# Strassen's scheme for feed-forward's first product of two blocks, in place of the output product of three

## The chip, the cores and the metric

The kernel runs on one core of a Trainium2 chip. The metric is the device time of one execution in microseconds (us), as the median of several runs. PE is the matrix engine, PEld its weight loads, DVE, ACT and POOL are the three elementwise engines, and SP issues the DMAs. PSUM is the accumulator memory that PE writes: 8 banks of 512 fp32 columns by 128 partitions. SBUF is the working memory.

## The reference

```python
attn_out = _attn_ref(q, k, v, f)            # 4 batches, 8 heads, 576 tokens, head size 64, decayed causal
x = attn_out.transpose(0, 2, 1, 3).reshape(2304, 512)
h = x @ w_in                                # 512 -> 2048       "feed-forward's first product"
g = np.maximum(0.01 * h, h)
x = g @ w_out                               # 2048 -> 512
h = x @ w_in2                               # 512 -> 1024       "layer 2"
e = np.exp(h - h.max(-1)); sm = e / (e.sum(-1) + 1e-09)
solu = h * sm
ln = (solu - mean(solu)) / sqrt(var(solu) + 1e-06) * g_ln
out = ln @ w_out2                           # 1024 -> 512       "the output product"
```

## The kernel before, in words

The 2304 tokens are 9 blocks of 256 (`TB`). Every product that has to be near fp32 is made of three fp16 matmuls: each operand is split into a high half and the rest, and high·high, high·low and low·high are summed in PSUM.

**Stages.** Attention runs over 16 pairs of heads. Feed-forward (`ffn`, L1056) takes one block and one half `g` of the hidden units: `hidden` (L1022) makes one 512-column PSUM bank per `k` (8 `k` in all, 4 in each half) with 24 matmuls of 256 columns, ACT and DVE make the activation and its two fp16 halves out of it, and then 4 times 24 matmuls of 256 columns make this half's share of `g @ w_out`, which is added into a tile `yo` and at last stored to HBM. `load_y` (L1091) reads such a block back and splits it, `layer2` (L1117) makes seven Strassen products out of it (L1124; 6 matmuls of 512 columns each) into the PSUM tiles `ph` (two banks each; two of them in all) and `ps_g`, and `normal` (L1166) does softmax and layer norm for each half `e` of the block (128 tokens): exp, a multiplication with its sum, a square with its sum, four small POOL instructions (`rstd`, L1183), an affine step.

**The output product** has two forms. The plain one (L1199 to L1218) splits the 128 normalised tokens, transposes the 2048 halves by one DMA, and runs 24 matmuls of 512 columns (`layer2_out`). For the last three blocks in order (`MIXED`, L87) `layer2_mix` (L1229) uses Strassen's scheme instead: both halves of the block are the rows, sums of their quarters are made on DVE and POOL, seven pieces are split and transposed by a DMA of 1024 each, and seven products of 12 matmuls of 256 columns are made (L1258) and combined by seven additions on DVE (L1275) after one copy on ACT (L1280). Its weights are mixed once, in `mixed_o` (L1002), on DVE, POOL and ACT.

**What sets the order.** The program is written as operations with a priority, a cost and the buffers they use (`Plan`, L148). `Plan.run` plays them against its cost table and writes out, for each engine, one fixed order of instructions; an operation that names several engines is given to one of them there. Constants such as `ORDER` (the order in which the blocks reach layer 2), `L2P`, `OUTP`, `PASSES` and `LD` are priorities or parts of them. Buffers have tags (`ps_f`: three PSUM banks; `ph`; `wz`: SBUF tiles of 128 by 512 fp32), and a tag that is no longer needed hands its tiles to another (`heirs`). On the chip each engine runs its order strictly, and waits where an input or a buffer isn't free.

Lines that many groups share are helpers: L529 is every matmul, L483, L488 and L490 are copies on ACT, DVE and POOL (`copy_on`), L494, L497 and L498 subtractions or additions (`sub_on`), L520 DMAs, L526 DMA transposes.

Of the kernel before, what the change touches and what calls it, by code (L numbers as in the profile page):

```python
# [30 lines left out]
ORDER = (0, 4, 1, 5, 3, 2, 6, 8, 7)  # L31
# [6 lines left out]
PASSES = (("A", 0, 127.52, 0.5), ("A", 1, 162.84, 3), ("B", 0, 200, 3.07), ("A", 2, 222, 8), ("B", 1, 234.49, 20), ("A", 3, 338, 8), ("B", 2, 372.93, 20), ("B", 3, 454.38, 15.2))  # L38
# [5 lines left out]
LD = -0.77  # L44
# [15 lines left out]
NWY = 12  # L60
NY2 = 2
NHL2 = 2
NTR = 3
PWL = 500.0
DMAR = 298.92
YB_ENGS = ("ACT",)
# [19 lines left out]
LNS = 256.0  # L86
MIXED = (6, 7, 8)  # L87
OMP = 931.77
# [37 lines left out]
WEIGHT2 = {"DVE": 1.93}  # L126
# [14 lines left out]
S_ENGS = ("POOL",)  # L141
O_ENGS = ("DVE", "POOL")
C_ENGS = ("ACT",)
NR2 = 1
# [266 lines left out]
def body(tc, kqa, kq, vt, f, wa, w2i, w2o, gln, out):  # L411
# [521 lines left out]
    def load_wi(k, prio):  # L933
# [7 lines left out]
        inverse(WS + k, ev(EK + k), ("w", k), ("k", k), prio)  # L941
# [114 lines left out]
    def ffn(blk, g, prio):  # L1056
        eprio = prio - EP
        first, last = blk not in YO, LEFT.setdefault(blk, 2) == 1
# [6 lines left out]
        gs = {k: hidden(k, XB[blk], prio + HST * i, eprio + i) for i, k in enumerate(GRP[g])}  # L1065
        for q in range(2):
            ps, yo = P.buf("ps_f"), YO[blk][q]
            for d in range(2):
# [6 lines left out]
                P.op(PE, 6 * len(GRP[g]) * mmr(TB), pe, prio + YD + 4 * q + 2 * d, r=list(gs.values()) + [WO[2 * k + i] for k in GRP[g] for i in range(2)],  # L1075
# [15 lines left out]
    def load_y(blk, prio):  # L1091
        yw, sy, y = P.buf("yw"), P.buf("sy"), P.buf("y2")
# [16 lines left out]
        pieces = [(512 * e, 512, lambda e=e: four(yw.t[:, 0:1024])[:, e::2], (yw, "e%d" % e)) for e in range(2)] + [(1024, 768, lambda: four(sy.t), sy)]  # L1109
        for at, n, v, k in pieces:  # L1110
            copy_f(lambda at=at, n=n: four(y.t[:, 0, at:at + n]), v, n, prio, scale=lambda: ev(IY + blk), w=[(y, (0, at))], r=[k, (EX, ("iy", blk))])
        for at, n, v, k in pieces:
            sub_f(lambda at=at, n=n: four(y.t[:, 1, at:at + n]), v, lambda at=at, n=n: four(y.t[:, 0, at:at + n]), n, prio, scale=lambda: ev(IY + blk),
                  w=[(y, (1, at))], rw=[k], r=[(y, (0, at)), (EX, ("iy", blk))])
        return y

    def layer2(tb, y, prio, oprios):  # L1117
# [7 lines left out]
        def prod(p, at, n, pr):  # L1125

            def pe():
                for k in range(2):
                    yh, yl = (y.t[:, j, at + 128 * k:at + 128 * k + 128] for j in range(2))
# [5 lines left out]
            P.op(PE, 6 * mmr(512), pe, pr, r=[y, W2I[0, n], W2I[1, n]], w=[p])  # L1135
# [24 lines left out]
        E = []  # L1160
# [249 lines left out]
```

## Time and profile before

| | |
|---|---|
| median of 3 runs | 749.15 us (748.75 to 750.18) |
| the profiled execution | 748.48 us, of which its span is 746.7 us |
| PE busy | 694.7 us, 93% of the span, 5711 matmuls |
| DVE, ACT, POOL busy | 534.6, 527.8, 393.6 us (72%, 71%, 53%) |
| mean granted clock of PE | 0.991 |

The span goes from the first to the last instruction; the 1.8 us between it and the execution's time lie outside. Matmuls overlap in the records (one of 256 columns is shown with 273 ns, but 24 of them in a row take 2.62 us), so the price of a matmul is read from a run of them, and not from its mean duration. A busy engine is not a bound one: what PE waits for, and where, is read from the waits and from the timeline.

### The profile page before, as it was taken

The page shows a single profiled execution, that of the slowest core. Times are in us where ns is not written, and L with a number is a line of the kernel's source. Part 1 is how long each engine was busy: PE and PEld are TensorE (multiplying, and loading weights), DVE is VectorE, ACT ScalarE, POOL GpSimd, SP SyncE. Part 2 cuts the span into 40 slices and gives each one's busy share as a digit, 9 for nine tenths or more (in the row PEclk, how much of TensorE's full clock was granted, in tenths as well). Part 3 has the DMA queues.
Part 4 walks back from the last instruction along what each step waited for, and adds up shares of the span by engine and source line. Part 5 has one row for each costly group of instructions (what it writes and reads, how often), then busy time and mean ns, then how long its engine had stood idle before and what let it go on. Part 6 is the DMA issues. An engine that isn't in the chain of part 4 may idle for free. (4 is left out here: it accounts for less than half of the span.)

```text
span 746.7 us, 15980 instructions
## 1 busy us (share of the span) xinstructions
PE 694.7 (93%) x5711; PEld 545.0 (73%) x5711; DVE 534.6 (72%) x1423; ACT 527.8 (71%) x1212; POOL 393.6 (53%) x503
## 2 busy tenths in 40 slices
PE   3368699999999999999999999999999999999997
PEld 2246488888888878888879888688856565444665
DVE  6998878888868787777975873341766774577873
ACT  4789989997988599989895754232744754457771
POOL 4557879794462075647521881020455865157661
PEclk9999699999999999999999999999999999999999
DMA  7999678647566675775965322010211335143666
GB/s 222 288 235 274 127 215 220 166 87 169 140 138 147 112 176 109 125 135 139 194 120 150 129 87 84 1 58 1 79 37 57 82 75 141 58 113 72 123 146 141
DMA packets 173599, 96.56 MB, mean 129 GB/s; under 512 B 153920, under 2 KB 153936, under 8 KB 173520
## 3 DMA queue, kind: packets, MB, share of 16 engines
q1 hardware_dynamic: 173488, 95.53, 54.2%
q8 instruction: 45, 0.74, 0.4%
q14 instruction: 34, 0.28, 0.1%
q10 hardware_dynamic: 32, 0.02, 0.0%
HBM read 47.95 MB, written 10.06 MB: 78 GB/s over the span
## 5 line engine op out<-in xcount | busy, mean ns | idle before, releaser
L529 PEld LDWEIGHTS <-wz 128*128 128x128 f16 x2904 | 281.4, 98 | 42.4 <-issue 6.7
L529 PE MATMUL ps_f<-g,wz 128*128 128x256 f16 x768 | 102.9, 276 | 0.0
L494 DVE SCALAR_TENSOR_TENSOR hl<-ps_s,st,hl 128x512 f16<-128x512 f32 (+4 forms) x160 | 82.1, 538 | 19.8 <-ACT hl L483 18.5
L529 PE MATMUL ps_f<-dec,wz 128*128 128x256 f16 x744 | 91.7, 273 | 0.0
L749 ACT ACTIVATE ps_s<-ps_s,st 128x512 f32<-128x512 f32 (+4 forms) x160 | 78.4, 490 | 13.2 <-DVE st L802 10.6
L498 POOL TENSOR_TENSOR kq<-raw,kq 64x576 fp32r<-64x576 f32 (+1 forms) x63 | 77.8, 1239 | 10.6 <-DMA pt<-hl 3.4
L483 ACT ACTIVATE hl<-ps_s,st 128x512 f16<-128x512 f32 (+4 forms) x153 | 74.8, 528 | 5.3 <-issue 1.6
L529 PE MATMUL ps_v<-pt,VT 128*128 128x128 f16 (+1 forms) x928 | 60.9, 217 | 18.9 <-DVE xr L836 12.3
L529 PEld LDWEIGHTS <-qa 128*128 128x128 f16 x696 | 67.5, 98 | 10.1 <-issue 1.4
L529 PEld LDWEIGHTS <-VT 128*128 128x128 f16 x928 | 53.5, 101 | 25.2 <-issue 9.4
L529 PE MATMUL ps_f<-x,wz 128*128 128x256 f16 x582 | 71.6, 276 | 0.0
L802 DVE CUSTOM_DVE_ANT_0 ps_s<-ps_s,mask 128x512 f32<-128x512 f32 (+3 forms) x128 | 62.4, 497 | 10.9 <-PE ps_s L529 9.1
L529 PEld LDWEIGHTS <-y 128*128 128x128 f16 x378 | 36.8, 98 | 45.7 <-issue 4.0
L529 PE MATMUL ps_s<-kq 128*128 128x512 f32 (+5 forms) x256 | 62.5, 375 | 0.9 <-DVE hl L494 0.4
L529 PEld LDWEIGHTS <-tr 128*128 128x128 f16 x348 | 33.9, 98 | 33.1
L529 PE MATMUL ps_f<-sd,wz 128*128 128x256 f16 x360 | 49.1, 273 | 0.0
L529 PEld LDWEIGHTS ps_s<-kq 128*128 128x128 f32 (+1 forms) x256 | 42.6, 197 | 6.7 <-DVE hl L494 1.0
L529 PE MATMUL ps_f<-wst,wz 128*128 128x256 f16 x366 | 47.1, 273 | 0.0
L836 DVE SCALAR_TENSOR_TENSOR xr<-ps_v,xr 64x256 f32<-64x256 f32 (+1 forms) x96 | 33.9, 353 | 14.8 <-ACT xr L833 13.2
L1037 ACT ACTIVATE ps_f<-ps_f 128x512 f32<-128x512 f32 x72 | 42.5, 590 | 0.3
L1038 DVE TENSOR_TENSOR g<-ps_f,g 128x512 f16<-128x512 f32 x40 | 27.5, 688 | 19.1 <-ACT ps_f L1037 18.8
L1038 DVE TENSOR_TENSOR dec<-ps_f,dec 128x512 f16<-128x512 f32 x32 | 22.0, 688 | 23.7 <-ACT ps_f L1037 23.2
(346 smaller groups left out, 1473.2 us busy)
## 6 DMA issues: line engine op xcount, KB each, us to landing
wst<-wa SPq DMA_DIRECT2D x32, 512.0 KB
raw<-kq SPq DMA_DIRECT2D x16, 480.0 KB
VT<-vt SPq DMA_DIRECT2D x16, 320.0 KB
raw<-yp_d SPq DMA_DIRECT2D x18, 256.0 KB
raw<-w2i SPq DMA_DIRECT2D x8, 512.0 KB
raw<-w2o SPq DMA_DIRECT2D x8, 512.0 KB
out<-ot SPq DMA_DIRECT2D x16, 256.0 KB
raw<-kqa SPq DMA_DIRECT2D x12, 256.0 KB
```

The source lines that it names most:

```text
L483: nc.scalar.activation(o, i, CP, scale=1.0 if scale is None else scale)
L494: nc.vector.scalar_tensor_tensor(o, a, scale, b, op0=ALU.mult, op1=ALU.subtract)
L498: (nc.vector if eng == DVE else nc.gpsimd).tensor_tensor(o, a, b, op=op)
L529: nc.tensor.matmul(o, lhsT=l, rhs=r, start=start, stop=stop)
L749: P.op(ACT, act(W, 1, True) + 93, lambda view=view, j=j, k=k: nc.scalar.activation(view(), view(), AF.Exp, bias=sts.t[:, j:j + 1], scale=- ...
L802: P.op(DVE, dve(W) + 130, lambda i=i, j=j, view=view: nc.vector.tensor_tensor_reduce(view(), view(), mask[:, 512 - 128 * i:640], -0.125, 3 ...
L836: P.op(DVE, dve(n) + 60, lambda: nc.vector.scalar_tensor_tensor(xr.t[a:a + 64, dst0:dst0 + n], ps.t[a:a + 64, c0:c1], PS, xr.t[a:a + 64, d ...
L1037: P.op(ACT, act(512, 0, True), lambda: nc.scalar.activation(ps.t, ps.t, AF.Prelu, scale=GS, alpha=0.01), eprio, rw=[ps])
L1038: P.op(DVE, dve(512) + 60, lambda: nc.vector.tensor_tensor(g.t[:, 1], ps.t, g.t[:, 0], op=ALU.subtract), eprio, w=[(g, 1)], r=[ps, (g, 0)])
```

## The change

Feed-forward's first product of blocks 6 and 7, which the order puts last, is made for both blocks together by Strassen's scheme (`hidden2`): the blocks are the two rows, the two halves of the 512 inputs the columns. Per `k` seven products of 6 matmuls of 256 columns replace 2 times 24 matmuls. One copy on ACT and seven additions on DVE combine them in one `ph` tile, and activation and split follow for each block. The weights' mixtures (`mixed_w`, per `k`) and the blocks' (`mixed_x`, once) are made ahead on DVE, POOL and ACT. `layer2_mix` and `mixed_o` are gone: the output product is plain for all nine blocks.

Tiles follow: `wt` holds the mixed weights and later becomes the tiles of the normalised halves and their transposes; `y2` becomes two tags; the second-layer weights are loaded after the last mixture is made (`deps`). Block 8 moves ahead of 6 and 7, and 1 ahead of 4. Some priorities and engine choices differ. Power-of-two scales differ too (`TOP2`, `GS`, `LNS`), which changes no instruction's size.

```diff
-ORDER = (0, 4, 1, 5, 3, 2, 6, 8, 7)
+ORDER = (0, 1, 4, 5, 3, 2, 8, 6, 7)
-... ("A", 2, 222, 8) ...
+... ("A", 2, 222, 9.78) ...
-LD = -0.77
+LD = 3.77
-NWY = 12
+NWY = 3
-YB_ENGS = ("ACT",)
+YB_ENGS = ("DVE", "ACT")
-MIXED = (6, 7, 8)
+PU = (((6, 7), 1), ((6, 7), 0))
-S_ENGS = ("POOL",)
+S_ENGS = ("DVE", "POOL")
...
-    def mixed_o(c, prio, after):
...
+    def mixed_w(k, prio, after):
+        za, zb, n, t = P.buf("wz"), P.buf("wz"), P.buf("wz"), P.buf("wt")
+        half = lambda z, h: lambda: z.t[:, 256 * h:256 * h + 256]
+        for z, c in ((za, 2 * k), (zb, 2 * k + 1)):
+            sub_f(lambda z=z: z.t, lambda c=c: W(WI[c], 0), lambda c=c: W(WI[c], 1), 512, prio, M_ENGS, op=ALU.add, w=[z], r=[WI[c]], deps=after)
+        sub_f(half(n, 0), half(zb, 1), half(zb, 0), 256, prio, M_ENGS, w=[(n, 0)], r=[zb])
...
+    def hidden2(k, p, prio, eprio):
+        X, Y, Z, u, ga, gb = P.buf("ps_f"), P.buf("ps_f"), P.buf("ph"), P.buf("hr"), P.buf("g"), P.buf("g")
...
+            def pe(o=o, xt=xt, w=w):
+                for d in range(2):
+                    wh, wl = (w(j)[:, 128 * d:128 * d + 128] for j in range(2))
+                    xh, xl = (xt()[:, j, TB * d:TB * d + TB] for j in range(2))
+                    mm(at(o)(), wh, xh, d == 0, False)
+                    mm(at(o)(), wh, xl, False, False)
+                    mm(at(o)(), wl, xh, False, d == 1)
...
+        plus(u2, P6, r1, w=[u2], r=[bank(P6), r1])
+        plus(u3, C22, u2, w=[u3], r=[bank(C22), u2])
+        plus(u2, P5, u2, rw=[u2], r=[bank(P5)])
+        plus(C22, P5, u3, rw=[bank(C22)], r=[bank(P5), u3])
+        plus(C21, C21, u3, rw=[bank(C21)], r=[u3])
+        plus(C11, C11, r1, rw=[bank(C11)], r=[r1])
+        plus(C12, C12, u2, rw=[bank(C12)], r=[u2])
+        for e, g in ((1, gb), (0, ga)):
...
+            P.op(ACT, act(512, 0, True), lambda g=g, row=row: nc.scalar.activation(g.t[:, 0], row(), AF.Prelu, scale=GS, alpha=0.01), eprio, w=[(g, 0)], r=ks)
+            P.op(ACT, act(512, 0, True), lambda row=row: nc.scalar.activation(row(), row(), AF.Prelu, scale=GS, alpha=0.01), eprio - 0.5 - 0.1 * e, rw=ks)
+            P.op(DVE, dve(512) + 60, lambda g=g, row=row: nc.vector.tensor_tensor(g.t[:, 1], row(), g.t[:, 0], op=ALU.subtract), eprio, w=[(g, 1)], r=ks + [(g, 0)])
...
     def load_w2i(k, h, prio):
         j = 2 * k + h
-        z = ZI[j] = whole(w2i[k, h], prio)
+        z = ZI[j] = whole(w2i[k, h], prio, None, mixed[-1:])
...
-            E.append(normal(2 * tb + e, blk, p, st, eprio, oprios[e], tb not in MIXED))
-        if tb in MIXED:
-            layer2_mix(tb, E[0], E[1], oprios[0], eprio)
+            normal(2 * tb + e, blk, p, st, eprio, oprios[e])
...
-    def layer2_mix(tb, e1, e2, oprio, eprio):
```

The change moves instructions on every engine. First VectorE, in the middle of feed-forward. Before, at the second half of block 7, these rows stand there: one 512-wide subtraction per `k` (L1038), among splits of the output weights (L494).

```order
L494 SCALAR_TENSOR_TENSOR wz_70<-wy_5612,ex,wz_70 128x512
L494 SCALAR_TENSOR_TENSOR wz_72<-wz_78,ex,wz_72 128x512
L1038 TENSOR_TENSOR dec_102<-ps_f_167,dec_102 128x512
L494 SCALAR_TENSOR_TENSOR wz_78<-wy_5613,ex,wz_78 128x512
L1038 TENSOR_TENSOR g_103<-ps_f_166,g_103 128x512
L494 SCALAR_TENSOR_TENSOR wz_75<-wst_98,ex,wz_75 128x512
L1142 ISA ph_5607,s_5636<-ph_5607,wst_99 128x512
L1142 ISA s_5636 128x1
L1038 TENSOR_TENSOR g_104<-ps_f_168,g_104 128x512
```

Now, at the pair of blocks 6 and 7 (L1105 is an addition of `hidden2`, 256 wide, out of PSUM; L1119 the subtraction; `hr` its partial sums):

```order
L1119 TENSOR_TENSOR dec_102<-ph_5562,dec_102 128x512
L1119 TENSOR_TENSOR dec_101<-ph_5562,dec_101 128x512
L1105 TENSOR_TENSOR hr_5584<-ph_5563,hr_5584 128x256
L1105 TENSOR_TENSOR hr_5584<-ps_f_168,hr_5584 128x256
L1105 TENSOR_TENSOR ph_5563<-ps_f_168,hr_5584 128x256
L1105 TENSOR_TENSOR ph_5563<-ph_5563,hr_5584 128x256 x3
L497 SCALAR_TENSOR_TENSOR wz_72<-qa,ex,wz_72 128x512
L1119 TENSOR_TENSOR g_106<-ph_5563,g_106 128x512
L1119 TENSOR_TENSOR g_103<-ph_5563,g_103 128x512
```

So a `k` of the pair has nine rows where two single blocks had two, and they come in a chain. The second place is POOL, just ahead of layer 2's first product, where the low halves of its mixed weights are made (two rows each: a scaling, L500, and a subtraction, L501). Ten such pairs stand there nearly in a row; four of them:

```order
L500 TENSOR_SCALAR wst_98<-wst_98,ex 128x512
L501 TENSOR_TENSOR wz_75<-wst_98,wz_75 128x512
L500 TENSOR_SCALAR wz_77<-wz_77,ex 128x512
L501 TENSOR_TENSOR sd_94<-wz_77,sd_94 128x512
L500 TENSOR_SCALAR wy_5567<-wy_5567,ex 128x512
L501 TENSOR_TENSOR wz_71<-wy_5567,wz_71 128x512
L500 TENSOR_SCALAR qa<-qa,ex 128x512
L501 TENSOR_TENSOR x_107<-qa,x_107 128x512
```

Before, six such pairs were POOL's share, and they stood much earlier. The third place is the end of SP's queue. Before, the transposes of `layer2_mix` (8 by 128 columns) and the stores of the output (`ot`):

```order
L526 DMA_TRANSPOSE qa<-hl_5627 128x8x128
L520 DMA out<-ot_5631 64x512
L526 DMA_TRANSPOSE tr_5629<-hl_5627 128x8x128
L526 DMA_TRANSPOSE tr_5629<-x_108 128x8x128
L520 DMA out<-ot_5632 64x512
L526 DMA_TRANSPOSE x_107<-hl_5626 128x8x128
L526 DMA_TRANSPOSE tr_5628<-qa 128x8x128
L520 DMA out<-ot_5631 128x512
L520 DMA out<-ot_5632 64x512
```

Now:

```order
L529 DMA_TRANSPOSE wt_5571<-wt_5572 128x16x128
L529 DMA_TRANSPOSE wt_5575<-wt_5576 128x16x128
L529 DMA_TRANSPOSE wt_5574<-wt_5572 128x16x128
L523 DMA out<-ot_5587 128x512
L529 DMA_TRANSPOSE wt_5577<-wt_5576 128x16x128
L523 DMA out<-ot_5588 128x512
L523 DMA out<-ot_5587 64x512 x2
L523 DMA out<-ot_5588 64x512 x2
```

Two transposes of 16 by 128 columns per block stand where seven of 8 by 128 stood, and more of the stores come behind the last transpose.

## Rows read from the trace of the kernel before

**Rows 1.** The page, parts 1 and 2: each engine's busy time; PE's and its clock's tenths, 40 slices.

```profile
span 746.7 us, 15980 instructions
...
PE 694.7 (93%) x5711; PEld 545.0 (73%) x5711; DVE 534.6 (72%) x1423; ACT 527.8 (71%) x1212; POOL 393.6 (53%) x503
...
PE   3368699999999999999999999999999999999997
...
PEclk9999699999999999999999999999999999999999
```

**Rows 2.** Stretches: us of the window, busy us (instructions) by engine, clock, DMA share, GB/s.

```profile
75.00:100.00 25.00, 18.49 (x121) 14.44 (x121) 19.80 (x58) 21.53 (x52) 19.95 (x21) 0.73 0.69 160
100.00:125.00 25.00, 25.00 (x245) 21.78 (x245) 21.84 (x61) 24.67 (x56) 21.28 (x22) 1.00 0.84 218
...
450.00:475.00 25.00, 25.00 (x220) 21.27 (x218) 7.05 (x10) 11.02 (x22) 2.91 (x4) 1.00 0.15 44
...
500.00:525.00 25.00, 25.00 (x232) 22.40 (x230) 6.88 (x13) 8.32 (x18) 1.61 (x2) 1.00 0.02 7
...
575.00:600.00 25.00, 25.00 (x167) 16.14 (x166) 19.87 (x51) 20.30 (x35) 21.68 (x29) 1.00 0.36 93
```

**Rows 3.** What PE waited for, from 455 us to the end: total us, times, longest.

```profile
PE ps_g L529 <- ACT wst L1152: 1.0, 1, 1.0
PE ph L529 <- DVE s L1142: 0.8, 2, 0.6
PE ps_g L529 <- DMA x<-hl: 0.6, 1, 0.6
PE ps_g L529 <- DVE ot L1275: 0.4, 1, 0.4
PE ph L529 <- DVE sd L1138: 0.2, 1, 0.2
PE ps_f L529 <- ACT wst L1280: 0.2, 1, 0.2
```

**Rows 4.** The same, from 100 to 455 us.

```profile
PE ps_v L529 <- DVE xr L836: 2.0, 3, 1.0
PE ps_s L529 <- DVE hl L494: 0.7, 2, 0.4
PE ps_v L529 <- ACT x L483: 0.4, 1, 0.4
PE ps_s L529 <- DVE st L764: 0.4, 1, 0.4
```

**Rows 5.** Chain of work that ended last: start us, us, what.

```profile
471.73 1.30 PE ps_g L529 x6
...
550.58 2.62 PE ps_f L529 x24
553.20 5.18 PE ps_g L529 x24
...
742.78 0.48 DVE ot L1275
```

**Rows 6.** Groups of instructions by line and shape: busy us, mean ns; then idle before.

```profile
L1037 ACT ACTIVATE ps_f<-ps_f 128x512 f32<-128x512 f32 x72 | 42.5, 590 | 0.3
...
L1038 DVE TENSOR_TENSOR g<-ps_f,g 128x512 f16<-128x512 f32 x40 | 27.5, 688 | 19.1 <-ACT ps_f L1037 18.8
...
L498 POOL TENSOR_TENSOR wz<-wz,wz 128x512 f16<-128x512 f32 x20 | 23.6, 1182 | 6.1 <-ACT wz L483 4.5
...
L497 POOL TENSOR_SCALAR wz<-wz,ex 128x512 f32<-128x512 f32 x26 | 20.9, 804 | 5.1 <-ACT wz L483 4.8
...
L1217 ACT ACTIVATE ot<-ps_f,ex 128x512 f32<-128x512 f32 x7 | 4.7, 677 | 8.5 <-PE ps_f L529 5.8 <-issue 2.8
```

**Rows 7.** L1275, L1280 and L1138: counts, duration ns min/median/max, first and last start.

```profile
L1275 DVE SCALAR_TENSOR_TENSOR ot<-ps_f,ex,wst x5: 473/476/484, 702.0 to 742.3; 128x256 f32<-128x256 f32 x5
...
L1280 ACT ACTIVATE wst<-ps_f,ex x2: 462/468/474, 698.1 to 719.9; 128x256 f32<-128x256 f32 x2
...
L1138 DVE TENSOR_TENSOR sd<-ph,sd x5: 682/691/692, 481.6 to 707.9; 128x512 f32<-128x512 f32 x5
```

**Rows 8.** L498 on DVE, both inputs in SBUF: the same columns.

```profile
L498 DVE TENSOR_TENSOR wz<-wz x4: 411/680/1647, 549.9 to 553.6; 128x512 f32<-128x512 f16 x3, 128x256 f32<-128x256 f32 x1
...
L498 DVE TENSOR_TENSOR hl<-raw,hl x13: 682/1221/1703, 534.2 to 723.1; 128x1024 f16<-128x1024 f32 x8, 128x512 f16<-128x512 f32 x5
```

More of the change, by code (lines that the diff above doesn't have):

```diff
@@ L125 @@
 WEIGHT = {"DVE": 6.79}
-WEIGHT2 = {"DVE": 1.93}
+WEIGHT2 = {"DVE": 2.58}
 HEAT = 0.25
@@ L140 @@
 LO_ENGS = ("DVE", "POOL")
-S_ENGS = ("POOL",)
-O_ENGS = ("DVE", "POOL")
-C_ENGS = ("ACT",)
-NR2 = 1
+S_ENGS = ("DVE", "POOL")
+M_ENGS = ("DVE", "POOL")
+MH_ENGS = ("ACT",)
 N_ENGS = ("DVE", "ACT")
@@ new lines, in mixed_x @@
+    def mixed_x(p, prio, after):
+        (a11, a12), (a21, a22) = XB[p[0]], XB[p[1]]
+        z11, z12, z21, n = (P.buf("wz") for _ in range(4))
+        x = lambda a, j: lambda: a.t[:, j]
+        v = lambda z: lambda: z.t
+        for z, a in ((z11, a11), (z21, a21), (z12, a12)):
+            sub_f(v(z), x(a, 0), x(a, 1), 512, prio, M_ENGS, op=ALU.add, w=[z], r=[a], deps=after)
+        sub_f(v(n), v(z11), v(z21), 512, prio, M_ENGS, w=[n], r=[z11, z21])
+        for j in range(2):
+            sub_f(v(z21), v(z21), x(a22, j), 512, prio, M_ENGS, op=ALU.add, rw=[z21], r=[a22])
+        sub_f(v(z11), v(z21), v(z11), 512, prio, M_ENGS, rw=[z11], r=[z21])
+        sub_f(v(z12), v(z12), v(z11), 512, prio, M_ENGS, rw=[z12], r=[z11])
+        out = []
+        for z in (z21, z11, n, z12):
+            t = P.buf("wz")
+            copy_f(lambda t=t: as_g(t.t)[:, 0], v(z), 512, prio, engs=MH_ENGS, w=[(t, 0)], r=[z])
+            sub_f(lambda t=t: as_g(t.t)[:, 1], v(z), lambda t=t: as_g(t.t)[:, 0], 512, prio, M_ENGS, w=[(t, 1)], r=[z, (t, 0)])
+            out.append(t)
+        SX[p] = out
@@ new lines, in ffn @@
+    def ffn(blks, g, prio):
+        eprio = prio - EP
+        if len(blks) == 1:
+            gs = [{k: hidden(k, XB[blks[0]], prio + HST * i, eprio + i) for i, k in enumerate(GRP[g])}]
+        else:
+            both = {k: hidden2(k, blks, prio + HS2 * i, eprio + i) for i, k in enumerate(GRP[g])}
+            gs = [{k: x[e] for k, x in both.items()} for e in range(2)]
+        for blk, gk, at in zip(blks, gs, (YD,) if len(blks) == 1 else PYS):
+            ffn_out(blk, g, gk, prio + at, eprio, 4 if len(blks) == 1 else QS)
@@ L1196, in normal @@
         flex(N_ENGS, [{DVE: dve2(1024) + 120, ACT: act(1024, 2)}[e] for e in N_ENGS], affine, eprio, rw=[Eb], r=[(st, 7)], lock=True)
-        if not plain:
-            return Eb
         hl, tr = P.buf("hl2"), P.buf("tr")
@@ L1317, in body @@
         nc.sync.dma_start(glt, gln)
-        for n, (blk, g) in enumerate(UN + tuple((blk, g) for blk in ORDER for g in range(2) if (blk, g) not in UN)):
-            ffn(blk, g, 1000.0 + US0 * n)
-            opened2 = [o for o in P.ops[-30:] if o.eng == PE][:1]
         def phase2():
@@ L1357, in body @@
         heirs("ps_f", "ps_g", "ps_g", "ps_g")
-        for c in range(NC2 // 2):
-            mixed_o(c, OMP + c, opened2)
         for tb in range(NB):
```

201 lines of the change are left out of this document (88 added, 113 removed).

## The prediction, made before the changed kernel ran

> **What bounds the kernel now.** I read the page's tenths first: from the fifth of 40 slices on PE shows 9 in nearly every slice while no other engine does, and its clock stands at full speed there [rows 1]. The stretches say the same in us: PE is busy 25.00 of 25.00 from 100 us on, while DVE, ACT and POOL may have much room (7, 11 and 3 us at 450 to 475) or little (20, 20 and 22 us at 575 to 600) without PE losing anything [rows 2]. Then the waits of PE: 3.5 us in all between 100 and 455 us, in attention [rows 4], and 3.2 us from there to the end [rows 3]. So after the start the time is PE's work plus some 7 us of small waits. What the change is worth is the PE work it takes away, the waits it removes, and the waits it makes. The start doesn't count: all engines' operations stand in the same order in both programs for about the first quarter of them, and what differs from there to the end of attention is where feed-forward's pieces stand between attention's.
>
> The price of a matmul comes from the chain, which shows runs without gaps: 24 of 256 columns in 2.62 us, 0.1092 us each, and 24 of 512 columns in 5.18 us, 0.2158 us each [rows 5]. Weight loads lie beside them: PEld is busy 545 us where PE is 695 [rows 1].
>
> **The change part by part.**
>
> *Feed-forward's first product of blocks 6 and 7.* Plain it is 2 times 24 matmuls per k, now 7 times 6 = 42. Six fewer for each of 8 k: 48 times 0.1092 = 5.24 us less on PE, which is on the path.
>
> *The output product of three blocks.* Before 7 times 12 = 84 matmuls of 256 columns each, 252 for three: 27.52 us. Now 2 times 24 of 512 columns, 144 for three: 31.08 us. 3.56 us more. PE's balance is -1.68 us.
>
> *Waits that go.* Three of PE's waits at the end belong to the Strassen output product: for its transposes (0.6), for its sums on DVE (0.4) and for its copy on ACT (0.2) [rows 3]. All three go, -1.2 us. What would be late next is the plain form of the last block: it needs exp, product, square, affine step, split and one long transpose before its output matmuls. The order puts four output tiles of older blocks, 4 times 5.18 = 20.7 us of PE work, between the last product of layer 2 and the last block's first half, and two more ahead of its second half (31 us in all), so I count nothing for it. On SP two transposes per block take the place of seven; the stores behind them aren't read by anyone.
>
> *The end.* The last thing before the final store was a DVE addition of 256 columns, 0.48 us [rows 5]; now it is an ACT copy of 512 columns, 0.68 us [rows 6]. +0.2 us. The store has the same size.
>
> *The mixing that goes and comes.* mixed_w and mixed_x put 28 additions of 512 columns and 21 of 256 on DVE, 16 and 11 on POOL, 20 copies on ACT. They stand beside plain feed-forward of blocks 2 and 8, where DVE and POOL had 18 us and more free in 25 (450 to 525 us) [rows 2]. Cost nothing there; without that cover, at 0.69 us [rows 7] and 1.18 us [rows 6] for a row of 512, they would be 30 us of DVE.
>
> *The sums of the pair: a new wait, (a).* One k costs DVE seven additions of 256 columns out of PSUM and two subtractions of 512. The trace has no such addition. Of 256 columns with a scale it has 0.476 us; without a scale but 512 wide 0.691 us, half of which is 0.35 [rows 7]. I take 0.45, near the row of the same width. 7 times 0.45 plus 2 times 0.688 [rows 6] is 4.53 us, against 42 times 0.1092 = 4.59 us on PE. ACT has 0.47 [rows 7] plus 4 times 0.59 [rows 6] = 2.8 us. So DVE is as long as PE wherever pairs' k follow each other, and it also has rows of the second layer's weights there. Only two `ph` tiles hold results, so PE may run two k ahead. The order puts 2.6 us pieces of block 8 between the first four k, then three k nearly in a row, and 10.5 us of second-product work (96 matmuls) behind them, in which DVE catches up. I count 0.5 us; the ends are 0 and 3.
>
> *Layer 2 starts later, (b).* Before, its first product came at 471.7 us [rows 5], between pieces of feed-forward. Now all of block 8 and the whole pair's first product, about 66 us of PE work by the prices above, stand ahead of it, and its weights are split just before it is reached: ten low halves in a row on POOL, each 0.80 plus 1.18 = 1.99 us [rows 6], 20 us, beside 17 us of PE work up to the first product and 26 us up to the last one that needs them. In the trace the same splitting ended without a wait of PE. I count 0.2 us; the ends are 0 and 2.
>
> *Layer 2 in less time, (c).* Its nine blocks had 2.0 us of waits (1.0, 0.8 and 0.2) [rows 3]. The second to fourth of the order now follow each other with 7.9 and 6.5 us of other PE work between the last product of one and the first that needs its `ph` tile; the later ones have 10.4 us, where three of them had 5.2. I count no difference; the ends are -2.0 and +3.
>
> *The rest:* block order, LD, PASSES, engine choices for the bounds and sums of y. They shift work among engines that aren't the bound, 3.5 us of attention's waits at most being at stake [rows 4]; I count 0, with 1.5 us either way.
>
> **Sum.** -5.24 + 3.56 - 1.2 + 0.2 + 0.5 + 0.2 = -1.98 us. The profiled execution took 748.48 us, span and 1.8 us around it; that makes 746.5. The median of the runs shown is 0.67 us higher, so the forecast is 747.2 us.
>
> *A rule against the change.* On DVE an addition of 512 columns (one of 256 among them) with both inputs in SBUF took from 0.41 to 1.65 us, with a median of 0.68 [rows 8], while an addition out of PSUM kept to 0.68 to 0.69 us [rows 7]. The Trainium skill, SBUF — State Buffer, section "Who interferes with whom", says why: a VectorE instruction with two SBUF inputs and a GpSimd instruction that reads SBUF share a port, and the second blocks until the first is done; with one SBUF input it doesn't. By that rule the seven additions are safe, but the weight rows that stand among them are not while POOL splits weights; a row so blocked delays the additions queued behind it. (a) would be 3 us or more, and the sum above zero; that is the first rival.
>
> **The rivals.**
>
> 1. *DVE becomes the bound in the pair's part.* The place is the eight k of blocks 6 and 7. It decides as soon as DVE needs more than 4.59 us per k on the average between two stretches of second-product work. At 0.476 us per addition and one further row of 0.75 us per k it is 7 times 0.476 + 1.38 + 0.75 = 5.46 us, 0.87 too much; times eight k 7 us of waiting on PE, half of it if the stretches between absorb the rest. For it: DVE is the queue with everything in it, and rows 8. Against it: the 10.5 us behind the three k in a row, in which DVE has little. Time: 747.2 + 3 to 6.5, 750.5 to 753.5 us. Chance 0.22.
> 2. *The gain is eaten in layer 2.* The two `ph` tiles are held from the product until softmax's multiplication; with closer blocks and a POOL that has the splits of the second layer's weights, (b) and (c) take 1 to 2.5 us more. 748.0 to 749.9 us. For it: before, blocks 5.2 us apart made 0.8 us of such waits [rows 3]. Against it: 575 to 600 us, where three engines were busy 20 of 25 us and PE lost nothing [rows 2]. Chance 0.20.
> 3. *Layer 2's waits go as well,* since its later blocks lie 10.4 us apart: 747.2 less 1.5 to 2, 745.2 to 745.7 us. Chance 0.08.
>
> That the change doesn't do what it says is ruled out by the order: PE has 156 matmuls fewer, 48 + 252 - 144.
>
> **How the numbers follow.** The forecast has 0.50, and its own range is 746.2 to 748.4 us. A measurement of this kernel can tell about 0.2%, 1.5 us. Faster than 747.65 is most of the forecast's range (0.38) and rival 3: 0.46. Within 0.2%: the forecast's upper part (0.12) and rival 2: 0.32. Slower: rival 1, 0.22. The range of 8 in 10 must reach into rival 1: 745.0 to 752.5 us leaves out about 0.06 below and 0.12 above.
>
> **What would show it.** PE with 5555 matmuls and about 1.7 us less work; no wait of PE in the last 30 us; for (a), the waits of PE on L1105 and L1119 between the first and the last product of the pair, below 1 us if I am right and 4 us or more for rival 1, with DVE without gaps there; for (b), a wait of the first products of layer 2 on the weight splits; for (c), waits of `ph` products on DVE rows of `normal`. Waits above 10 us in all after attention would make the forecast wrong, and so would attention ending more than 2 us earlier or later.

## The result, and the profile after

The changed kernel takes 756.37 us (median of 9 runs, 752.04 to 758.45), the kernel before 749.35 us in the runs beside it. The ratio is 1.0083, with a 95% interval of 1.0066 to 1.0100: slower by 5 to 7.5 us. The forecast was 747.2 us, the range ended at 752.5, and rival 1 (750.5 to 753.5 us) had the sign but not the size. The profiled execution took 756.44 us. The first two parts of its page, against [rows 1]:

```profile
span 754.6 us, 15677 instructions
...
PE 695.9 (92%) x5555; PEld 530.1 (70%) x5555; DVE 534.9 (71%) x1450; ACT 541.6 (72%) x1230; POOL 429.3 (57%) x525
...
PE   3367699999999999999999999999899999999997
...
PEclk9999799999999999999999999999999999999999
```

156 matmuls are gone, as they should be, and yet PE is busy 1.2 us longer and idle 6.7 us longer (754.6 - 695.9 against 746.7 - 694.7). The tenths of PE differ in two slices, a 7 in the fourth (an 8 before) and an 8 at 528 to 547 us (a 9 before); the clock is as it was but for one tenth in the fifth slice. Both kernels by stretches, first before, then after (columns: the stretch, its length, then busy time and instructions of PE, PEld, DVE, ACT, POOL, the granted clock, the DMA share, GB/s). They end at 407 us, where attention is done in both, at 545, where the changed kernel starts layer 2, and at 680:

```profile
0.00:100.00 100.00, 59.13 (x329) 45.51 (x330) 84.37 (x254) 78.08 (x211) 64.36 (x83) 0.93 0.89 231
100.00:407.00 307.00, 303.27 (x3003) 266.76 (x3003) 243.01 (x728) 271.06 (x694) 169.91 (x220) 1.00 0.68 148
407.00:545.00 138.00, 137.79 (x1220) 119.06 (x1218) 71.20 (x138) 68.95 (x132) 51.96 (x57) 1.00 0.21 66
545.00:680.00 135.00, 133.06 (x761) 74.31 (x760) 89.09 (x201) 70.91 (x117) 73.88 (x101) 1.00 0.29 73
680.00:760.00 80.00, 61.45 (x407) 39.39 (x404) 46.90 (x107) 38.77 (x60) 33.51 (x44) 0.99 0.53 112
```

```profile
0.00:100.00 100.00, 57.81 (x308) 44.07 (x309) 83.31 (x250) 76.04 (x206) 63.31 (x83) 0.93 0.91 227
100.00:407.00 307.00, 303.01 (x2996) 265.66 (x2994) 239.08 (x730) 266.86 (x692) 168.06 (x214) 1.00 0.65 140
407.00:545.00 138.00, 133.34 (x1216) 118.66 (x1214) 99.45 (x187) 75.23 (x147) 78.02 (x77) 1.00 0.17 56
545.00:680.00 135.00, 131.56 (x721) 70.24 (x719) 89.68 (x227) 89.83 (x143) 95.63 (x120) 1.00 0.44 110
680.00:760.00 80.00, 70.19 (x324) 31.51 (x322) 23.41 (x61) 33.63 (x47) 24.25 (x34) 0.98 0.33 73
```

PE's idle time in the pair's stretch goes from 0.21 to 4.66 us, with DVE idle for 39 of 138 us there, and in layer 2 from 1.94 to 3.44. Idle time isn't all, since the same clock time holds different work. So I count the matmuls that start behind a time, by width, and take 0.1092 us for 256 columns and 0.2158 for 512 [rows 5]. What the clock shows beyond this work, up to the last matmul (742.74 and 750.49 us), is loss:

| | before | after | difference, us |
|---|---|---|---|
| work in the whole program | | | -1.68 |
| work left at 407 us: matmuls of 256 and 512 columns | 1704, 666: 329.80 us | 1433, 810: 331.28 us | 1.48, where -1.68 was due: 3.16 behind |
| loss 407 to 545 (the pair) | 0.75 | 5.98 | +5.23 |
| loss 545 to 680 (layer 2) | 2.98 | 5.23 | +2.25 |
| loss 680 to the last matmul | 2.21 | 1.00 | -1.21 |
| last matmul to the span's end | 3.96 | 4.13 | +0.17 |

The first row is contained in the second. From the second row on the differences add up to 7.92 us, the difference of the two spans. The waits of PE from 455 us to the end, against [rows 3]:

```profile
PE ph L532 <- DVE hr L1105: 2.6, 4, 1.1
PE ph L532 <- DVE s L1218: 2.1, 6, 0.9
PE ph L532 <- DVE ph L1105: 2.0, 1, 2.0
PE ph L532 <- DVE raw L1249: 0.8, 2, 0.5
PE ps_g L532 <- ACT wst L1228: 0.7, 1, 0.7
PE ph L532 <- DVE ex L705: 0.2, 1, 0.2
```

The two rows on L1105, 4.6 us in five waits, are the place and the size that I had named for rival 1. The first of them in the timeline of the changed kernel:

```profile
475.23 0.82 PE L532 MATMUL ph<-wst,qa 128*128 128x256 f16 x6
...
476.08 0.42 DVE L1105 TENSOR_TENSOR hr<-ph,hr 128x256 f32<-128x256 f32 x1 [0.58 <-PE ph L532]
476.54 0.43 DVE L1105 TENSOR_TENSOR hr<-ps_f,hr 128x256 f32<-128x256 f32 x1
476.56 0.81 PE L532 MATMUL ph<-wy,qa 128*128 128x256 f16 x6 [0.52 <-DVE hr L1105]
...
477.88 1.37 DVE L1105 TENSOR_TENSOR ph<-ph,hr 128x256 f32<-128x256 f32 x3
```

It doesn't look like an overloaded DVE: DVE had itself been idle for 0.58 us, waiting for PE. The product that waits is `C12`, the last of the k, which writes columns 256 to 511 of its `ph` tile. The addition that it waits for is `u3 = C22 + u2`, which reads columns 768 to 1023 of the same tile, in the other bank. No value passes between them. The recorded order has `u3` ahead of `C12`, and the semaphores that are made from it treat the tile as one. In the five k with a wait an addition of this kind stands ahead of the product (in the fifth, with 2.0 us, three of them); in the other three k behind it.

### The profile page after: what moved, and what is told of

It reads as the page before. It is cut to its first block, busy times and chain, and to the rows that moved or that the text cites. A ratio compares the mean times of both kernels' runs of the same rounds, so it can differ in the third digit from the quotient of the medians.

```text
span 754.6 us, 15677 instructions
## 1 busy us (share of the span) xinstructions
PE 695.9 (92%) x5555; PEld 530.1 (70%) x5555; DVE 534.9 (71%) x1450; ACT 541.6 (72%) x1230; POOL 429.3 (57%) x525
## 4 chain that ended last, share of the span: by engine, by line
PE 46%; DVE 7%; ACT 2%; issue 1%; POOL 0%; POOLq 0%; DVEq 0%; ACTq 0%
PE ps_f L532 32%; PE ph L532 6%; PE ps_g L532 5%; PE ps_s L532 2%; PE ps_v L532 1%; DVE raw L1249 1%; DVE wst L1214 1%; DVE ph L1105 1%; DVE ph L1218 1%; DVE hr L1105 1%; ACT ph L1118 0%; DVE raw L501 0%; DVE g L1119 0%; DVE sd L1214 0%; ACT g L1117 0%
## 5 line engine op out<-in xcount | busy, mean ns | idle before, releaser
L532 PEld LDWEIGHTS <-wz 128*128 128x128 f16 x2628 | 255.3, 99 | 42.7 <-issue 11.1
L532 PE MATMUL ps_f<-g,wz 128*128 128x256 f16 x924 | 120.0, 276 | 0.0
L532 PEld LDWEIGHTS <-wt 128*128 128x128 f16 x720 | 70.2, 98 | 65.0 <-issue 1.8
L497 DVE SCALAR_TENSOR_TENSOR hl<-ps_s,st,hl 128x512 f16<-128x512 f32 (+4 forms) x160 | 82.2, 539 | 20.9 <-ACT hl L486 19.6
L501 POOL TENSOR_TENSOR kq<-raw,kq 64x576 fp32r<-64x576 f32 (+1 forms) x63 | 77.0, 1227 | 6.8 <-ACT kq L486 3.6
L532 PE MATMUL ps_v<-pt,VT 128*128 128x128 f16 (+1 forms) x928 | 61.1, 218 | 19.5 <-DVE xr L839 10.9
L532 PE MATMUL ps_f<-dec,wz 128*128 128x256 f16 x588 | 74.7, 273 | 0.0
L532 PE MATMUL ps_f<-x,wz 128*128 128x256 f16 x432 | 55.6, 281 | 0.0
L501 POOL TENSOR_TENSOR wt<-raw,wt 128x1024 f16<-128x1024 f32 (+1 forms) x22 | 43.7, 1995 | 5.8 <-ACT wt L486 5.2
L839 DVE SCALAR_TENSOR_TENSOR xr<-ps_v,xr 64x256 f32<-64x256 f32 (+1 forms) x96 | 33.9, 353 | 12.2 <-ACT xr L836 10.4
L532 PE MATMUL ps_f<-wz,wt 128*128 128x512 f16 x174 | 40.0, 379 | 0.0
L493 POOL TENSOR_SCALAR kq<-raw 64x960 fp32r<-64x960 f32 x22 | 22.0, 1001 | 30.9 <-PE ps_s L532 26.0
L836 ACT ACTIVATE xr<-ps_v 64x256 f32<-64x256 f32 (+1 forms) x96 | 31.2, 325 | 10.9 <-PE ps_v L532 4.0
L1243 ACT ACTIVATE raw<-ph,s,ex 128x1024 f32<-128x1024 f32 x18 | 21.6, 1202 | 23.5 <-DVE s L1242 18.9
```

The costliest lines, as they stand in the source:

```text
L493: nc.gpsimd.tensor_scalar(o, i, 1.0 if scale is None else scale, 1.0, op0=ALU.mult, op1=ALU.mult)
L497: nc.vector.scalar_tensor_tensor(o, a, scale, b, op0=ALU.mult, op1=ALU.subtract)
L501: (nc.vector if eng == DVE else nc.gpsimd).tensor_tensor(o, a, b, op=op)
L532: nc.tensor.matmul(o, lhsT=l, rhs=r, start=start, stop=stop)
L836: P.op(ACT, act(n, 1, True), lambda: nc.scalar.activation(xr.t[a:a + 64, dst0:dst0 + n], ps.t[b:b + 64, c0:c1], CP, scale=PS), prio, w=[(x ...
L839: P.op(DVE, dve(n) + 60, lambda: nc.vector.scalar_tensor_tensor(xr.t[a:a + 64, dst0:dst0 + n], ps.t[a:a + 64, c0:c1], PS, xr.t[a:a + 64, d ...
```

## The experiments

Ratios are against runs of the kernel before that were made beside them on the same chip; its medians there are 748.7 to 749.7 us. Programs that ran beside different ones are better compared by their ratios than by their medians.

### The pair: E1, E8, E13

E1 lets `u3`, when its turn comes, write `C12` first if that hasn't been written.

```diff
+            if i == 6:
+                held = [pe]
+                pe = last = lambda: held and held.pop()()
             P.op(PE, 6 * mmr(TB), pe, prio + 0.2 * i, ...)
...
-        plus(u3, C22, u2, w=[u3], r=[bank(C22), u2])
+        plus(u3, C22, u2, last, w=[u3], r=[bank(C22), u2])
```

> The changed kernel with one thing moved: in each k of the pair the seventh product (C12, columns 0 to 511 of its ph tile) is written ahead of the addition that reads C22 (columns 512 to 1023 of the same tile), so that it no longer waits for it; the other engines keep their order. Theory A (the five waits of PE on L1105, 4.6 us, come from that order and from nothing else): these waits fall below 0.5 us, PE's idle time between 472 and 545 us falls by 4 to 5.5 us, and the time is 4 to 5.5 us below the changed kernel's, 750.5 to 752.5 us. Theory B (my rival 1, DVE is the bound in the pair's part): the products start earlier but the following k then wait for DVE; at least 3 us of waits stay in the pair's part and the time is 0 to 1.5 us below, 754.5 to 757 us.

Measured (E1): 751.03 us, 1.0020 (1.0004 to 1.0036), 5.3 us below the changed kernel by the medians, 4.7 by the ratios. The same place in E1's timeline, all waits of PE from 407 to 545 us, and that stretch:

```profile
474.88 0.82 PE L532 MATMUL ph<-wst,qa 128*128 128x256 f16 x6
...
475.54 0.82 PE L532 MATMUL ph<-wy,qa 128*128 128x256 f16 x6
...
476.39 0.42 DVE L1108 TENSOR_TENSOR hr<-ph,hr 128x256 f32<-128x256 f32 x1 [1.24 <-PE ph L532]
```

```profile
PE ps_f L532 <- DVE hr L1108: 0.8, 1, 0.8
PE ps_g L532 <- DVE va L682: 0.7, 1, 0.7
PE ph L532 <- DVE g L1122: 0.7, 1, 0.7
```

```profile
407.00:545.00 138.00, 135.75 (x1230) 120.14 (x1229) 98.89 (x189) 75.83 (x147) 78.92 (x78) 1.00 0.16 56
```

The product follows its neighbour without a gap, and the waits on the additions from `ph` are gone. What appears is smaller and of another kind: a bank, a value and a tile that DVE gives late, 2.2 us. Theory A holds for the seen waits and for the time, but not for PE's idle time: that was to fall by 4 to 5.5 us and falls by 2.4, from 4.66 to 2.25. By the count of matmuls the pair's loss goes from 5.98 to 3.27 us. E12 and E9, below, differ by the same edit and ran side by side: 3.3 us by the medians, 3.7 by the ratios, and a loss of 5.88 and 3.53 us. So the order is worth 2.4 to 2.7 us in the pair's stretch of the profiles and 3.3 to 5.3 us of time. Where the rest of the time is gained stays open; a profile is one execution.

Nor does E1 untie the two: now the addition waits for the product (1.24 us idle before it, where it was 0.58), and over the eight k DVE's waits for PE ahead of `u3` rise from 8.5 to 10.5 us. A tile of its own for each bank might untie them; no run tried it. The Trainium skill, PSUM — Partial Sum Buffer, section "PSUM bank collisions raise a hardware error", asks that two engines be kept apart by bank and quarter of the partitions; by that, too, a product in one bank need not wait for an addition in the other. E1 doesn't show this, since its addition starts (476.39 us) when the product has ended.

E8 asks whether DVE has room behind that:

```diff
-... nc.vector.tensor_tensor(g.t[:, 1], row(), g.t[:, 0], op=ALU.subtract), ...
+... [nc.vector.tensor_tensor(g.t[:, 1], row(), g.t[:, 0], op=ALU.subtract) for n in range(2)], ...
```

> E1 with each of the pair's sixteen subtractions of 512 columns on DVE (L1119 of the changed kernel, 0.69 us each) issued twice: 11 us more work on DVE in the pair's stretch and nothing else. It repeats a step and changes no value. If DVE is the bound there (rival 1), the time rises by 6 us or more, above 757 us. If DVE has room (it was busy 51 of 74 us between 472 and 546 us in the changed kernel), by less than 3 us, under 754 us.

Measured (E8): 761.94 us, 1.0168 (1.0152 to 1.0183), 10.9 us above E1: it was paid in full. Its waits of PE from 455 to 560 us, and two stretches:

```profile
PE ph L532 <- DVE g L1122: 2.4, 1, 2.4
PE ps_f L532 <- DVE hr L1108: 2.3, 1, 2.3
PE ps_g L532 <- DVE va L682: 2.1, 2, 1.5
PE ps_f L532 <- DVE g L1022: 1.3, 1, 1.3
PE ph L532 <- DVE x L497: 1.3, 1, 1.3
```

```profile
500.00:515.00 15.00, 12.06 (x109) 10.46 (x107) 13.39 (x32) 7.69 (x16) 9.20 (x8) 0.99 0.44 153
515.00:525.00 10.00, 10.00 (x79) 8.38 (x79) 5.84 (x15) 3.65 (x7) 0.69 (x1) 0.85 0.16 55
```

9.4 us are waits for DVE, 7.0 more than E1 has from 455 us on of these kinds. Part of the rest is the clock: after a stretch in which PE was busy 12.06 of 15 us, the granted clock of the next 10 us is 0.85 (part of it at 1.2 GHz in place of 2.4). So the order's waits were one thing, and close behind them DVE's chain is a second limit. E13 takes time off that chain without moving anything, on E9 (E1 with the kernel before's `LD` and `PASSES`, below):

```diff
-... nc.vector.tensor_tensor(at(o)(), at(a)(), at(b)(), op=ALU.add) ...
+... nc.vector.tensor_tensor(at(o)()[:, :64], at(a)()[:, :64], at(b)()[:, :64], op=ALU.add) ...
```

> E9 with the pair's seven additions per k made on 64 of their 256 columns; the rest of the sums is left out, so the values are wrong from there on. The order of every engine is E9's; DVE has about 56 times 0.2 to 0.3 us less to do, 11 to 17 us, all in the pair's chain. If DVE's chain sets the pace there (as E8's full price for added work says), PE's idle time from 407 to 545 us falls from 3.5 to under 2 us and the time is 1.5 to 3 us below E9's 749.3 us, 746.3 to 747.8 us. If what is left there is not DVE's (starts of runs, ps_g's single matmuls), the time is within 0.7 us of E9's.

Measured (E13): 747.29 us, 0.9977 (0.9966 to 0.9989), 2.0 us below E9 by the medians, 1.7 by the ratios. The pair's stretch in E9 and in E13:

```profile
407.00:545.00 138.00, 135.51 (x1213) 118.44 (x1212) 100.18 (x191) 75.42 (x146) 78.97 (x77) 1.00 0.16 56
```

```profile
407.00:545.00 138.00, 137.56 (x1230) 120.13 (x1229) 93.72 (x194) 76.64 (x150) 80.76 (x78) 1.00 0.16 57
```

PE's idle time falls from 2.49 to 0.44 us, and the loss from 3.53 (the 3.5 of the expectation is this one) to 0.82, next to 0.75 in the kernel before. So by the profiles the pair's loss of 5.98 us has two causes of about the same size: 2.7 us go with the order (E1), and 2.7 us more with the length of the additions (E13). DVE was idle for 38 of 138 us in E9 even so: what counts is how long a product waits for its chain, not how full DVE is. That two `ph` and three `ps_f` tiles let PE run only so far ahead would explain it; no run changed their number.

### Attention's order: E12, E11, E9, E6, E4

```diff
-LD = 3.77
+LD = -0.77
-... ("A", 2, 222, 9.78) ...
+... ("A", 2, 222, 8) ...
```

E12 makes this edit in the changed kernel, E9 in E1, E6 in E5 (below). E11 is the reverse edit in the kernel before; E4 adds the changed kernel's `ORDER` to that. Theory L says that these two constants cost 1.5 to 2.5 us. Of the start, the first 100 us, theory S says that its difference is chance, and theory D that it belongs to the changed kernel.

> The changed kernel with the kernel before's LD and PASSES alone, the pair's waits kept. Theory L: 1.5 to 2.5 us below the changed kernel, 754 to 755 us, and the five waits on L1105 (4.6 us) as in the changed kernel. If the loss was chance: 755.5 to 757 us.

Measured (E12): 752.64 us, 1.0049 (1.0032 to 1.0066); the waits on L1105 are still 2.6 and 2.0 us. By the medians it is 3.7 us below the changed kernel, more than theory L had, and by the ratios 2.5.

> The kernel before with the changed kernel's LD and PASSES alone, the order of blocks kept. Theory L: 1.5 to 2.5 us above the kernel before, and E4's smaller loss of 1.0 means that the order of blocks gave some of it back. If the loss was chance: within 0.5 us of the kernel before.

Measured (E11): 750.12 us, 1.0022 (1.0010 to 1.0034), 1.2 us above the kernel before by the medians, 1.6 by the ratio.

> E1 with the kernel before's LD and PASSES, layer 2 as in the changed kernel. Four profiles with the changed kernel's LD and PASSES beside two with the kernel before's, by the work that is left at 407 us (matmuls times the price from the chain), put the loss at some 2 us; E6 against E5 said 1.7. Theory L (these two constants cost 1.5 to 2.5 us): 748.5 to 749.5 us, equal to the kernel before. If the loss was chance: 750.5 to 751.5 us, as E1.

Measured (E9): 749.34 us, 1.0000 (0.9987 to 1.0012), 1.7 us below E1 by the medians, 1.5 by the ratios.

> E5 with the kernel before's LD and PASSES, which set where loads and attention's pieces stand up to 400 us; the order of blocks stays the changed kernel's. If LD and PASSES carry the 1.0 us (0.2 to 2.3) by which E4 was slower than the kernel before: 0.5 to 1.5 us below E5, 748 to 749.5 us, and the place in the work at 407 us is 0.5 to 1.5 us further. If they carry nothing (that was the order of blocks, or chance in the start): within 0.5 us of E5.

Measured (E6): 751.03 us, 1.0032 (1.0021 to 1.0043), 1.7 us below E5 by the medians, 1.2 by the ratios.

> The kernel before with the changed kernel's LD, PASSES and ORDER alone (what moves feed-forward's pieces between attention's, and the order of blocks in layer 2). My sum counted 0 with 1.5 us either way: 747.8 to 751 us. If the loss of some 3 us before the end of attention belongs to these three edits, 752 us or more, with 3 us more of PE's idle time before 407 us. Its first 100 us are the kernel before's in order: 330 to 334 matmuls by theory D, 312 to 335 by theory S.

Measured (E4): 750.71 us, 1.0017 (1.0002 to 1.0031), not to be told from E11.

All five point the same way: theory L, 1.2 to 2.5 us by the ratios. They don't say which of the two constants it is, and E4 has `ORDER` with them. The work left at 407 us says it once more, each program's own total allowed for: 327.7 to 330.9 us in the nine profiles with `LD = -0.77` (mean 329.5), 330.7 to 333.0 in the seven with 3.77 (mean 331.5). If each profile's own start, the time at which its 341st matmul began, is taken off, the two groups no longer overlap (226.8 to 228.7 and 229.0 to 230.4), and their means are 1.8 us apart. Where between 100 and 407 us it is lost the profile doesn't say: PE is idle 3.7 us there before and 4.0 after.

The rest of the 3.16 us is the start, and chance. At the 341st matmul the changed kernel's profile is already 2.2 us behind that of the kernel before (103.47 and 101.28 us), yet all programs have the same order up to some 208 us, and in 16 profiles, one of each program, PE began 308 to 340 matmuls in the first 100 us. The changed kernel's 308 is the lowest, E7's 340 the highest:

```profile
0.00:100.00 100.00, 59.21 (x340) 46.02 (x341) 86.08 (x255) 79.23 (x214) 64.10 (x83) 0.95 0.87 231
```

Two programs of the changed kernel's start gave 334 and 337 (E3, E14). In the changed kernel's profile a DMA at 33 us landed 1.1 us later than before; that the lag comes from it isn't shown. Theory D fell.

### The parts alone: E2, E3

```diff
-MIXED = (6, 7, 8)
+MIXED = ()
```

> The kernel before with MIXED empty: the output product is plain for all nine blocks, nothing else is changed. By the terms of my sum: +3.56 us of PE work, -1.2 us of waits of the mixing, +0.2 us at the end, 2.6 us above the kernel before, about 752 us (ratio 1.0035). If the plain form of the last block makes a wait of its own, 754 us or more; if the mixing cost more than its waits show, 750.5 us or less. Its first quarter is the kernel before's own, so its profile is also a second look at the start: if the start's difference between the two kernels is chance (theory S), its first 100 us may hold 312 to 335 matmuls; if it belongs to the changed kernel (theory D), 330 to 334 as before.

Measured (E2): 753.35 us, 1.0057 (1.0036 to 1.0077): 4.3 us by the ratio and 3.7 by the medians, not 2.6. In its profile the loss behind 680 us is 1.1 us smaller, as I had counted, but that from 545 to 680 us is 1.7 us larger (4.71, where it was 2.98). One wait there grew: PE on L1152's copy, 2.4 us where it was 1.0 [rows 3]. So the Strassen output product was probably worth more than my sum had it (the interval is 2.7 to 5.8 us).

```diff
-PU = (((6, 7), 1), ((6, 7), 0))
+PU = ()
...
-L2P = (..., 1388.69, 1381.8, ...)
+L2P = (..., 1381.8, 1388.69, ...)
```

> The changed kernel without the pair: feed-forward's first product is plain for all blocks (PU empty; the tiles that the mixed weights held go to their heirs at once; two priorities of L2P are exchanged). +5.24 us of PE work against the changed kernel, less its waits at the pair (4.6 us and the restart behind each, 5 us together): 756 to 757 us, no difference, if layer 2 keeps its waits. If the mixing of weights and blocks ahead of the pair also costs something, it is faster than the changed kernel, 753 to 755 us; if the pair's waits only stand for others, 760 to 762 us. Its start is the changed kernel's own: by theory D 310 to 314 matmuls in the first 100 us, by theory S anything from 312 to 335.

Measured (E3): 764.57 us, 1.0200 (1.0182 to 1.0219), worse than all cases named. The profile shows a long wait in layer 2, which is no price of the pair:

```profile
PE ph L532 <- DVE raw L1249: 11.0, 3, 9.3
```

```profile
590.00:600.00 10.00, 0.81 (x4) 0.29 (x3) 9.48 (x18) 6.44 (x9) 7.09 (x8) 0.78 0.37 72
600.00:606.00 6.00, 5.89 (x15) 2.08 (x15) 3.25 (x8) 3.67 (x5) 4.03 (x7) 0.52 0.55 144
```

In the new order layer 2 waits 9.3 us for a `ph` tile, and PE, busy for 0.81 of 10 us, works at a granted clock of 0.52 in the next 6, nearly all of it at 1.2 GHz. The run is inconclusive on what was asked.

### Layer 2 and the spacing: E5, E7, E10, E14

The waits on L1218 are of the same kind: a product into one half of a `ph` tile behind a DVE row on the other half. E5 (on E1) and E7 (on the kernel before) write both such products ahead, E10 (on E9) only the one whose place among PE's matmuls doesn't change by it:

```diff
+        first = lambda p: tb and p == (p2, 1) and held[p2, 0]()
...
+            if p == (p2, 0):
+                todo = [pe]
+                pe = held[p] = lambda: todo and todo.pop()()
```

with `first(p)` called ahead of the row in `plus` and `full`.

> E1 and, in layer 2 of all blocks but the first, the same edit: a product into one half of a ph tile is written ahead of the additions (L1214, L1218 of the changed kernel) that read the other half. Theory A2 (these waits, 2.1 us in the changed kernel, 0.9 in E1's profile, come from the whole tile being one thing to the waits): no wait of PE on L1214 or L1218 for a ph product, PE's idle time between 560 and 680 us falls from 4.4 to under 3.5 us, and the time is 0.5 to 2 us below E1's 751.0 us, 749 to 750.5 us. Theory C (the buffers, two ph tiles held until softmax's multiplication, make layer 2's loss): the waits move to L1249 and the time stays within 0.4 us of E1's.

Measured (E5): 752.73 us, 1.0048 (1.0033 to 1.0064), 1.7 us above E1 by the medians, where theory A2 had it below. The loss from 545 to 680 us is 7.2 us where E1 has 4.6.

> The kernel before with the edit of layer 2 of E5 alone: products into the other half of a ph tile ahead of the additions, for all blocks but the first. The kernel before had 0.8 us of such waits of PE (L1142), so by theory A2 0.5 to 1 us is gained: 748.5 to 749.2 us, and the waits on L1142 are gone. By theory C no gain: 749.3 to 750 us.

Measured (E7): 757.16 us, 1.0116 (1.0099 to 1.0133), 8 us slower. In both, these waits are gone, but the edit also puts the product of `x4` ahead of the one of `x1` that the sums need next. E7 has eight kinds of waits that the kernel before hasn't, and the one for a copy of `layer2_mix` grew from 0.2 [rows 3] to 2.7 us. They say nothing on the whole-tile wait.

> E9 with a narrower form of E5's edit: in layer 2 only the product into the first half of the second ph tile is written ahead of the two DVE rows that read the other half; the order of PE's matmuls is then the same as E9's, which it was not in E5 and E7 (there another product was put ahead of the one that the sums need next). Theory A2 (the waits on L1218 at this product, 2.1 us in the changed kernel and 0.9 in E1, are waits for the whole tile and nothing else): they vanish, and the time is 0.5 to 2 us below E9's. Theory C (the two ph tiles are held, another wait takes their place): within 0.4 us of E9's.

Measured (E10): 751.31 us, 1.0036 (1.0023 to 1.0049), 2 us above E9. PE's waits from 545 us on in E9, then in E10:

```profile
PE ph L532 <- DVE s L1221: 1.9, 5, 0.9
PE ph L532 <- DVE raw L1252: 0.8, 2, 0.5
PE ps_g L532 <- ACT wst L1231: 0.7, 1, 0.7
```

```profile
PE ps_g L532 <- DVE va L682: 1.4, 1, 1.4
PE ph L532 <- DVE raw L1258: 1.0, 3, 0.5
PE ps_g L532 <- ACT wst L1237: 0.7, 1, 0.7
PE ps_f L532 <- DMA wt<-wt: 0.6, 1, 0.6
PE ps_f L532 <- DVE va L682: 0.6, 1, 0.6
PE ps_f L532 <- DVE s L1251: 0.4, 1, 0.4
```

The 1.9 us are gone, and 3.2 us of other waits have come. The loss behind 545 us rises from 6.3 to 7.3 us. So theory A2 falls, and theory C is right in kind but not in size, since it had the time unchanged. As far as this one edit tells, PE is ahead of DVE in layer 2 whatever it is made to wait for. The instructions of PE, DVE, ACT and POOL have the same order in both programs from start to end, so only the places of the waits differ. Of the 2 us the profiles show about 1; where the other is stays open.

```diff
-HS2 = 7.26
+HS2 = 9.0
```

> E9 with HS2 = 9 in place of 7.26, which sets the distance of the pair's k in priority: the order of feed-forward's pieces changes, and the first block of layer 2 comes ahead of the pair's last k. If the rest of the pair's idle time goes with more distance: 747 to 748.8 us, under the kernel before. If the order only shifts the waits (ph tiles shared by the last k and by layer 2): 749.5 to 753 us.

Measured (E14): 754.40 us, 1.0092 (1.0073 to 1.0111). More distance put the first block of layer 2 ahead of the pair's last k, and PE waited 2.9 us for `ph` tiles and 2.5 us for a `ps_g` tile; the clock was 0.92 to 0.93 from 545 to 568 us. This spacing shifts the waits. No version ran below the kernel before with the whole computation; E9 equals it.

## Why the prediction was wrong, step by step

- **PE's work, -1.68 us: right by the count,** 5555 matmuls. **Waits of the mixing, -1.2: right,** the loss behind 680 us fell by 1.21, and by 1.1 in E2. **(b), layer 2's start: right,** no wait ended on the weight splits. **The end, +0.2:** the 0.17 is luck, since the time behind the last matmul is 3.77 to 4.14 us in the twelve profiles with the plain end and 3.79 to 5.08 in the four with the other.
- **(a), the sums of the pair, 0.5 with ends 0 and 3: wrong, +5.2 us.** This step failed most. It compared totals, whether DVE has the time in one k (4.53 us against 4.59), and let PE run two k ahead and DVE catch up behind. It took each addition's duration rightly: three took 1.37 us, 0.46 each. It did not ask which instruction waits for which. By the profiles half of the loss comes from the order: a product waited for an addition that it has no value from, because both touch one tile and the recorded order has them that way round. E1 takes 2.7 us of loss away with it (4.7 to 5.3 us of time). The other half is the chain: with the additions made short and nothing moved, E13 takes away 2.7 us of loss (1.7 to 2.0 us of time). The clue to the first was in my own rows: 0.8 us of `ph` products waiting on L1142, a DVE row on the other half of the tile [rows 3]; I read it as a tile that comes free late.
- **Rival 1** had the place, the sign and a price of 3 to 6.5 us, but only half of the mechanism: I had asked for "DVE without gaps there", and it was idle for 39 of 138 us. DVE's chain is the second half: E13 shows its price, and E8 that nothing is left for more. The rule that I cited for it, the Trainium skill, SBUF — State Buffer, "Who interferes with whom", agrees with the weight rows in that stretch, two SBUF inputs each: the same row of 512 columns took 0.68 us at 481.62, with no POOL row beside it, and 1.48 at 505.44, beside additions on POOL. But these rows were hardly what PE waited for: from 472 to 546 us the 512-column rows of L914 and L497 took 2.2 us more than at their shortest in the changed kernel, and 3.3 us in E13, where PE's idle time is nearly gone.
- **The rest, 0 with 1.5 either way: wrong, 3.16 us.** I let attention's order count for nothing because PE's waits there were small. `LD` and `PASSES` cost 1.2 to 2.5 us, in five comparisons; by what mechanism stays open. In the profiled execution a late start was added by chance.
- **(c), layer 2 in less time, 0 with ends -2 and +3: off by 2.25 us,** inside its ends. The waits on L1218 rose from 0.8 (L1142 before) to 2.1 us; E10 took such waits out of E9, and others came.
- **The plain output product: mis-sized.** Alone it costs 4.3 us (2.7 to 5.8) where I had 2.6, with 1.7 us of loss in layer 2 that the sum didn't have.
- **Readings of the rows** that were looser than written, with no weight in the sum: from 100 us on PE is busy for as little as 23.80 of 25 us in the stretches not shown, PE and its clock are full from the sixth slice and not the fifth, and DVE had 14.9 us free from 475 to 500 us, not 18. The sign that I had set, waits above 10 us after attention, would have missed the loss: the waits are 8.4 us and the loss is 12.2.

So without the order's waits and `LD` the forecast of a small gain still fails: E9 is at 0 in place of -2. In its profile the pair still loses 2.8 us more than the kernel before did there, and layer 2 2.5 us more. What the pair alone is worth no run says, since E3, which was to say it, failed by another wait.

## What to carry to other kernels

A scheme that saves matmuls by sums pays in instructions that read the accumulators, and each such row can hold a product that needs nothing of it: for every tile that two engines share, list in the recorded order what stands ahead of what, and count a wait wherever a write follows a read of the same tile, whatever the columns. When a wait is taken away, look at what stands next in line before counting the gain: here 3 to 5 us came back in the pair, where DVE was only just behind, and nothing in layer 2, where other waits took the place. A busy share doesn't tell: DVE was idle for 38 of 138 us, and still its chain cost some 2 us. Small constants that move the order of a full engine are worth a run of their own.

## What was not expected of the hardware

The start varies by itself: with one order of instructions, in 16 programs, PE began 308 to 340 matmuls in the first 100 us, and the 341st began between 100.0 and 103.5 us, so that single profiles can differ there by 3.5 us. And idle time can be paid twice: after 9.3 us of waiting in E3 the granted clock was 0.52 for 6 us, and after some 3 us of idle time within 15 in E8 it was 0.85 over 10 us. The five waits of 0.5 to 2.0 us in the changed kernel left it at 1.00 in the profiled execution. The three longest of its nine runs (757.30 to 758.45 us) had a mean granted clock of 0.988, the others 0.990 to 0.993; why isn't known, as they weren't profiled.
